# Token pairs for batch 0's V, heads paired two apart, and new orders of work in a fused attention and MLP kernel

## The chip, the cores and the metric

The kernel runs on one core of a Trainium2 chip. The metric is device time in microseconds. Before the change the median of three runs was 214.91 us (214.89 to 215.71). A core has a matrix engine (TensorE, PE in the profile; its weight loads are PEld), VectorE (DVE), ScalarE (ACT), GpSimd (POOL) and SyncE (SP). [...]

## The reference

Four batches, eight heads, 768 tokens, 64 elements a head. Tokens go in chunks of 32; a chunk's queries see 16 tokens to the left, the chunk, 8 to the right, and 8 memory tokens.

```python
for c in range(nc):
    q_c = q[:, :, c_start:c_end]
    k_full = concat([mem_k, k[:, :, l_start:r_end]]); v_full = ...
    a = softmax(scale * q_c @ k_full.T)
    out[:, :, c_start:c_end] = a @ v_full
x = out.transpose(0, 2, 1, 3).reshape(B * S, H * D)   # 3072 x 512
h = x @ w_in                                          # 512 x 2048
g = h + sin(alpha * h) ** 2 / (alpha + 1e-9)
return g @ w_out                                      # 2048 x 512
```

## The kernel before

**Stages.** A prologue (stage -1) does batch 0's attention; stages 0 to 3 then do the MLP of one batch each, and within stages 0 to 2 the next batch's attention. The order of all work is written by hand as strings of words (L813 for the prologue, L821 on for the stages); a word is a letter and its arguments, and `Stage.run` (L525) calls `do_<letter>`. The framework puts in the waits but moves nothing: every engine works its instructions in the order of the words. PSUM has 8 banks; `Banks` (L59) hands out pairs and single banks by the order in which they were given back.

**Blocks.** Three chunks make a block of 96 queries; a batch has 8 blocks. A block's keys are 128 rows: 64 tokens from 16 before the block, 8 memory tokens, 56 further tokens. For batches 1 to 3 the words are by block: `s` scores and exp (`scores`, L379), `v` values (`values`, L408) and normalizing (`normed`, L350), then the block's 96x512 result is turned for the MLP either by PE and a copy (`t` copy on DVE, `T` on ACT; `turned`, L362) or by a DMA transpose on SP's queue (`c`, L624).

**Batch 0** goes by head pair and half of the sequence instead (words `s01`, `v01`, `T01`: pair, half). k and q of two neighbouring heads at a time are loaded as f32 by eight DMAs on SP (L708), cast to bf16 by ACT or DVE (`a`, L653), transposed by PE (`k`, `l`; `turn`, L269) and copied into kT and qT (`K`, `L`; `put_k`, L282, with the sequence's two ends always by DVE, L291; `put_q`, L297). `u_scores` (L314) first puts the mask into PSUM with two 64x128x384 matmuls (L317) and then adds, per block, one matmul a head with 64 rows (the head's elements) and 128 columns (the keys) (L325); one 128x768 exp follows on ACT (L332). `u_values` (L339) multiplies the 128 keys by V with a column of ones (128x65, L344), the ones giving the softmax's sum. DVE takes the reciprocal (L353) and multiplies (L354); `u_turn` (L372) transposes four blocks of a pair by PE (L366) and copies them into xT (L369).

**V** lies in vw with a key on each partition: GpSimd loads it with 256 bytes a token and head, cast to bf16, as 64 token rows (L172) and 56 (L179), two to four heads at a time (`V`); the memory rows are loaded once for all batches (memv_st, L665, word `dm`) and copied into batch 0's V by DVE (`m0`, L188). GpSimd's DMAs use eight completion semaphores in turn, so its ninth waits until its first has landed.

**MLP.** `b` and `h` are the two halves of a tile of 128 of the 2048 hidden columns: four matmuls of 384 tokens each (`half_tile`, L422), over the four 128-row chunks of xT; then sine on ACT (L439), square on ACT, DVE or POOL (`q`, L441), gT on DVE (`g`, L451). The second product is fed in between, one 512-column matmul at a time (`f`, L462). `p` and `P` start a tile's first or second half early (`early`, L533). `I` and `U` load the weights, `R` and `X` a later batch's k and q by rows and their DMA transposes, `z` are fillers that keep PE busy, `W` loads ACT's table early, `C` sets up constants.

Of the kernel before, what the change touches and what calls it, by code (L numbers as in the profile page):

```python
# [17 lines left out]
ALU = mybir.AluOpType  # L18

# [66 lines left out]
def kernel(  # L86
# [42 lines left out]
    tiny = consts.tile([1, 1], F32, name="tiny")  # L129
    zeros = consts.tile([P, 512], BF, name="zeros")  # L130
# [3 lines left out]
    xslots = Slots([consts.tile([QW, HP, 2, D], BF, name=f"x_blk{i}") for i in range(6)])  # L134
    NPT = 8
    pts = [consts.tile([P, H * QW + 32], BF, name=f"pt{i}") for i in range(NPT)]
    memv_st = consts.tile([P, B, H, D], BF, name="memv_st")
    kst = consts.tile([P, NJ, H * D], BF, name="kst")
# [5 lines left out]
    memk_st = memv_st[96:104].rearrange("n b h d -> n b (h d)")  # L144
    memkT = consts.tile([P, HP, NK], BF, name="memkT")
# [13 lines left out]

    def load_v(b, h0, h1):  # L160
# [5 lines left out]
        lo = c0  # L166
        if c0 == 0 and b == 0:
            nc.gpsimd.dma_start(vw[16:64, 0:1, 0:D], vf[0:48, 0:1])
            lo = 1
        a = base + QW * lo - 16  # L170
        n = c1 - lo
        nc.gpsimd.dma_start(  # L172
            vw[0:64, lo:c1, 0:D], win(vflat, a, n, 64)
        )
# [94 lines left out]
    def turn(src, hp):  # L269
        bank, bs = banks.single()  # L270
        t = bank[:, 0:384].bitcast(BF).rearrange("p (r c) -> p r c", r=6)
        for r in range(6):
            for e in range(2):
                nc.tensor.transpose(
                    t[64 * e:64 * e + 64, r, :], src[:, 2 * hp + e, r, :], ident[:]
                )
        return t, bs

# [35 lines left out]
    def u_scores(b, hp, half):  # L314
# [7 lines left out]
        for i in range(4):  # L322
            j = 4 * half + i
            for e in range(2):
                nc.tensor.matmul(  # L325
                    t[:, e, QW * i:QW * i + QW],
                    kTs[b % 2][64 * e:64 * e + 64, hp, 104 * j:104 * j + P],
                    qTs[b % 2][64 * e:64 * e + 64, hp, QW * j:QW * j + QW],
                    start=False, stop=(i == 3),
                )  # L330
        pt = next_pt()
        nc.scalar.activation(  # L332
            pt[:, 0:H * QW].rearrange("p (e c) -> p e c", e=2), t[:, :, 0:HALF],
# [5 lines left out]
    def u_values(b, hp, half, pt):  # L339
        ot, bs = banks.pair()  # L340
        otv = ot[:, :, 0:4 * (D + 1)].rearrange("p e (g c) -> p e g c", c=D + 1)
        for e in range(2):
            for i in range(4):
                nc.tensor.matmul(  # L344
                    otv[:, e, i, :], pt[:, HALF * e + QW * i:HALF * e + QW * i + P],
                    vws[b % 2][:, 2 * hp + e, 4 * half + i, 0:D + 1],
                )
        return normed(otv, bs)

    def normed(otv, bs):  # L350
        rinv = blk.tile([QW, 2, HP], F32, name="rinv")
        x_blk = xslots.take()
        nc.vector.reciprocal(rinv[:], otv[0:QW, :, :, D])  # L353
        nc.vector.tensor_tensor(  # L354
            out=x_blk[:].rearrange("p g e d -> p e g d"), in0=otv[0:QW, :, :, 0:D],
# [4 lines left out]
        return x_blk  # L360
# [11 lines left out]
    def u_turn(xT, hp, half, x_blk, eng="V"):  # L372
        turned(
            x_blk,
            xT[:, hp, HALF * half:HALF * half + HALF].rearrange("p (g c) -> p g c", g=4), eng)
# [32 lines left out]
    def values(b, j, pt):  # L408
        ot, bs = banks.pair()
        otv = ot[:, :, 0:4 * (D + 1)].rearrange("p e (g c) -> p e g c", c=D + 1)  # L410
        for e in range(2):
            for hp in range(HP):
                i = 4 * e + hp
                nc.tensor.matmul(  # L414
                    otv[:, e, hp, :], pt[:, QW * i:QW * i + P],
                    vws[b % 2][:, 2 * hp + e, j, 0:D + 1],
                )
        return normed(otv, bs)
# [82 lines left out]
    todo = [(hp, half) for hp in range(HP) for half in range(2)]  # L501

    class Stage:
# [29 lines left out]
        def early(self, a, hf):  # L533
            if int(a) not in self.tile:
                self.tile[int(a)] = opened(int(a), self.next_x() if self.i < 0 else self.xT)
            t = self.tile[int(a)]
            half_tile(t, hf, 0, 3)
            t["from"][hf] = 3
# [46 lines left out]
        def do_k(self, a):  # L585
            self.piece["k" + a] = turn(k_bf, int(a))

        def do_l(self, a):
            self.piece["q" + a] = turn(q_bf, int(a))
# [13 lines left out]
        def do_v(self, a):  # L603
            if self.b == 0:
                self.xb[a] = u_values(0, int(a[0]), int(a[1]), self.pt.pop(a))
# [3 lines left out]
        def turn_x(self, a, eng):  # L609
            x = self.next_x()  # L610
            x_blk = self.xb.pop(a)
            if self.b == 0:
                u_turn(x, int(a[0]), int(a[1]), x_blk, eng)
            else:
                turned(x_blk, x[:, :, QW * int(a):QW * int(a) + QW], eng)
# [8 lines left out]
        def do_c(self, a):  # L624
            if self.b == 0:
                c0 = HALF * int(a[1])
                x = self.next_x()[:, int(a[0]), c0:c0 + HALF].rearrange("p (g c) -> p g c", g=4)
            else:
                c0 = QW * int(a)
                x = self.next_x()[:, :, c0:c0 + QW]  # L630
# [6 lines left out]
        def do_V(self, a):  # L637
            b, h0, h1 = (int(c) for c in a)
            load_v(b, h0, h1)

        def do_m(self, a):
            put_memv(int(a))

# [6 lines left out]
        def do_a(self, a):  # L650
            hp = int(a[0]) % HP
            dst = kq[int(a[0]) // HP]
            copier(a[1])(  # L653
                dst[:, 2 * hp:2 * hp + 2].rearrange("p h r d -> p h (r d)"), kq_f[int(a[0])][:]
# [8 lines left out]
        def do_d(self, a):  # L663
            if a == "m":
                nc.gpsimd.dma_start(memv_st[64:72].rearrange("n b h d -> n (b h) d"),  # L665
                                    mem_v.rearrange("b h n d -> n (b h) d"))
            elif a == "y":
# [5 lines left out]
            else:  # L673
                src, dst = (k, k_bf) if a[0] == "k" else (q, q_bf)
                load_one(src, dst, int(a[1]), int(a[2]), int(a[3]))
# [27 lines left out]
    kq_f = [mlp.tile([P, 2, 6 * D], F32, name="kq_f", tag=t) for t in ("u", "s2") * 4]  # L703
# [3 lines left out]
    def load_f(src, hp, t):  # L707
        nc.sync.dma_start(  # L708
            t[:], src[0, 2 * hp:2 * hp + 2].rearrange("h (p r) d -> p h (r d)", p=P)
        )  # L710

    load_f(k, 0, kq_f[0])
    load_f(q, 0, kq_f[4])
    for bb in range(B):
        if not CROSSED[bb][0]:
            nc.scalar.dma_start(memk_f[NM * bb:NM * bb + NM], mem_k[bb].rearrange("h n d -> n h d"))
    nc.scalar.dma_start(alpha_rows[:], moe_alpha.rearrange("(ft p) -> ft p", p=P))
    for hp in (1, 2, 3):
        load_f(k, hp, kq_f[hp])
        load_f(q, hp, kq_f[4 + hp])  # L720
    nc.vector.memset(zeros[:], 0.0)
    nc.vector.memset(tiny[:], 0.0)
    nc.vector.memset(mcol[:], 0.0)
    masks.make_identity(nc, ident[:])
    for vw in vws:
        nc.gpsimd.memset(vw[0:32, 0, 0, 0:D], 0.0)
        nc.gpsimd.memset(vw[96:128, H - 1, NJ - 1, 0:D], 0.0)
# [22 lines left out]
    def const_m():  # L750
# [3 lines left out]
        nc.vector.tensor_copy(mrow[:], mt)  # L754
# [11 lines left out]
    def const_k():  # L766
        nc.vector.tensor_copy(memk_bf, memk_f[0:NK])
# [30 lines left out]

    def const_v():
# [3 lines left out]
    def const_s():  # L803
# [4 lines left out]
                     s=const_s, z=const_z)  # L808
# [64 lines left out]
```

## Time and profile before

| | |
|---|---|
| median of three runs | 214.91 us |
| the profiled execution | 214.84 us, of which the span is 213.1 |
| TensorE clock granted | 1.0 |
| first MLP matmul (L424) of the unbroken stream | 24.81 us from the start |
| end of the last matmul group | 210.28 |
| DMA: software queue, hardware queue of SP | 13.25 MB in 68736 packets, 14.62 MB in 26976 |

A line of the page names an engine, an operation, the tiles it writes and reads, their shapes, and the number of instructions; behind the bar stand the time that the group was busy, the mean of one in ns, and the engine's idle time just before them with what ended it. A tile's name is that of the program. Slices are fortieths of the span, 5.3 us each, with the busy share in tenths. The chain of work is followed back from the end: each piece is what released the next one. In the DMA list the last number is the median from issue to landing.

### The profile page before, as it was taken

To read this page: it belongs to the slowest core of one execution; us is meant where nothing else is said; L and a number is where in the kernel's file an instruction comes from. 1 tells how busy PE (TensorE), PEld (TensorE's weight loads), DVE (VectorE), ACT (ScalarE), POOL (GpSimd) and SP (SyncE) were. 2 spreads that over 40 slices of the span, in tenths; PEclk is the share of its full clock that TensorE was granted. 3 is DMA by queue.
4 is the path that set the end of the run, shared out by engine and by line. 5 is a ranking of instruction groups with operands and counts; after the bars stand their busy time and mean duration, and the time that the engine had idled before them with its cause. 6 is when DMAs were issued, how large, how long until landed. Compare 5 with 4: busy or idle time off the path is not lost.

```text
span 213.1 us, 4479 instructions
## 1 busy us (share of the span) xinstructions
PE 201.7 (95%) x1721; PEld 113.5 (53%) x1721; DVE 140.5 (66%) x218; ACT 143.5 (67%) x230; POOL 99.8 (47%) x140
## 2 busy tenths in 40 slices
PE   0799899999999999999999999999999999999994
PEld 0456555565455556555455555554555555554443
DVE  7598678999542749975856649898157197865011
ACT  2597898976857469977846199887846289891110
POOL 8959515688598193009991039659400023200000
PEclk9999999999999999999999999999999999999999
DMA  6999999999999999969999229989945400000312
GB/s 195 337 163 141 193 209 205 204 163 182 131 177 141 137 148 144 180 88 110 126 217 171 72 63 131 156 126 129 175 115 123 124 15 0 2 3 0 148 49 98
DMA packets 95908, 28.19 MB, mean 132 GB/s; under 512 B 84864, under 2 KB 92432, under 8 KB 95888
## 3 DMA queue, kind: packets, MB, share of 16 engines
q0 software_dynamic: 68736, 13.25, 92.3%
q1 hardware_dynamic: 26976, 14.62, 28.2%
q8 instruction: 13, 0.21, 0.4%
q14 instruction: 7, 0.06, 0.1%
q10 hardware_dynamic: 176, 0.04, 0.1%
HBM read 29.66 MB, written 6.29 MB: 169 GB/s over the span
## 4 chain that ended last, share of the span: by engine, by line
PE 71%; DVE 9%; DMA 7%; ACT 4%; issue 4%; POOL 3%; DVEq 0%; POOLq 0%; ACTq 0%
PE ps L462 38%; PE ps L424 27%; DMA memv_st<-in_mem_v_dram 4%; DVE gT L451 4%; DVE s L447 3%; DMA vw<-in_v_dram 3%; PE ps L414 3%; PE ps L385 2%; ACT u L439 2%; PE ps L366 1%; ACT s L444 1%; POOL s L447 1%; POOL vw L172 1%; DVE kT L285 1%; ACT L699 1%
## 5 line engine op out<-in xcount | busy, mean ns | idle before, releaser
L462 PE MATMUL ps<-w_out_sb,gT 128*128 128x512 bf16 (+2 forms) x400 | 89.1, 371 | 0.0
L424 PE MATMUL ps<-xT,w_in_sb 128*128 128x384 bf16 x512 | 86.0, 326 | 0.7 <-DVE gT L451 0.4
L451 DVE SCALAR_TENSOR_TENSOR gT<-s,inv_alpha,ps 128x768 bf16<-128x768 f32 x64 | 63.0, 1011 | 12.5 <-ACT s L444 5.2
L424 PEld LDWEIGHTS <-w_in_sb 128*128 128x128 bf16 x512 | 49.8, 98 | 35.4 <-issue 2.1
L439 ACT ACTIVATE u<-ps,alpha_sb 128x768 f32<-128x768 f32 x64 | 56.6, 895 | 16.8 <-PE ps L424 14.3
L462 PEld LDWEIGHTS <-gT 128*128 128x128 bf16 x400 | 36.6, 98 | 37.9 <-DVE gT L451 0.2
L447 POOL TENSOR_TENSOR s<-u 128x768 f32<-128x768 f32 x11 | 17.4, 1582 | 69.7 <-ACT u L439 69.7
L399 ACT ACTIVATE pt<-ps,biasm 128x256 bf16<-128x256 f32 x72 | 27.2, 489 | 10.5 <-PE ps L385 10.5
L469 DVE COPY o_sb<-ps 128x512 f32<-128x512 f32 (+1 forms) x15 | 10.1, 678 | 28.3 <-PE ps L462 26.4
L447 DVE TENSOR_TENSOR s<-u 128x768 f32<-128x768 f32 x23 | 21.9, 953 | 7.8 <-ACT u L439 7.8
L444 ACT ACTIVATE s<-u 128x768 f32<-128x768 f32 x30 | 25.0, 841 | 0.5
L354 DVE TENSOR_TENSOR x_blk<-ps,rinv 96x512 bf16<-96x512 f32 x32 | 22.0, 687 | 1.1
L469 ACT COPY o_sb<-ps 128x512 f32<-128x512 f32 (+1 forms) x10 | 5.6, 562 | 21.6 <-PE ps L462 21.6
L172 POOL DMA_DIRECT2D vw<-in_v_dram x13 | 12.9, 994 | 7.9 <-PE ps L366 5.4
L353 DVE RECIPROCAL rinv<-ps 96x8 f32<-96x8 f32 x32 | 6.4, 200 | 13.5 <-PE ps L414 12.7
L179 POOL DMA_DIRECT2D vw<-in_v_dram x13 | 12.7, 976 | 0.0
L238 POOL DMA_DIRECT2D kst<-in_k_dram x16 | 12.2, 760 | 1.1 <-DMA vw<-in_v_dram 0.8
L232 POOL DMA_DIRECT2D kst<-in_k_dram x16 | 11.3, 708 | 2.3 <-DMA vw<-in_v_dram 1.6
L369 ACT COPY xT<-ps 128x384 bf16<-128x384 bf16 x12 | 5.6, 496 | 8.2 <-PE ps L366 8.2
L245 POOL DMA_DIRECT2D q_bf<-in_q_dram x12 | 10.7, 912 | 0.0
L414 PEld LDWEIGHTS <-pt 128*128 128x128 bf16 x192 | 8.2, 97 | 4.2 <-ACT pt L399 0.3
L414 PE MATMUL ps<-vw,pt 128*128 128x65 bf16 x192 | 8.9, 193 | 0.0
(81 smaller groups left out, 131.4 us busy)
## 6 DMA issues: line engine op xcount, KB each, us to landing
out_dram<-o_sb SPq DMA_DIRECT2D x23, 256.0 KB, 2.3
kq_f<-in_k_dram SPq DMA_DIRECT2D x4, 384.0 KB, 6.5
kq_f<-in_q_dram SPq DMA_DIRECT2D x4, 384.0 KB, 6.0
q_bf<-in_q_dram POOLq DMA_DIRECT2D x12, 128.0 KB, 6.7
w_in_sb<-in_moe_w_in_dram POOLq DMA_DIRECT2D x1, 1152.0 KB, 12.6
vw<-in_v_dram POOLq DMA_DIRECT2D x7, 128.0 KB, 6.7
vw<-in_v_dram POOLq DMA_DIRECT2D x8, 112.0 KB, 7.4
kst<-in_k_dram POOLq DMA_DIRECT2D x14, 64.0 KB, 5.1
```

What stands on the lines that cost most here:

```text
L172: nc.gpsimd.dma_start(vw[0:64, lo:c1, 0:D], win(vflat, a, n, 64))
L179: nc.gpsimd.dma_start(vw[72:128, c0:hi, 0:D], win(vflat, base + QW * c0 + 48, hi - c0, 56))
L354: nc.vector.tensor_tensor(out=x_blk[:].rearrange("p g e d -> p e g d"), in0=otv[0:QW, :, :, 0:D], in1=rinv[:].unsqueeze(3).to_broadcast([Q ...
L399: nc.scalar.activation(pt[:, 0:H * QW].rearrange("p (g e c) -> p g e c", g=2, e=4)[:, :, :, 32 * m:32 * m + 32], sc[:, :, 0:4 * QW].rearra ...
L414: nc.tensor.matmul(otv[:, e, hp, :], pt[:, QW * i:QW * i + P], vws[b % 2][:, 2 * hp + e, j, 0:D + 1],)
L424: nc.tensor.matmul(t["hT"][:, hf, 0:HALF], w_in_sb[:, kt, P * t["ft"]:P * t["ft"] + P], t["xT"][:, kt, HALF * hf:HALF * hf + HALF], start= ...
L439: nc.scalar.activation(t["u"][:], t["hT"][:, :, 0:HALF], ACTF.Sin, scale=alpha_sb[:, ft:ft + 1])
L444: nc.scalar.activation(s2[:], u[:], ACTF.Square)
L447: e.tensor_tensor(out=s2[:], in0=u[:], in1=u[:], op=ALU.mult)
L451: nc.vector.scalar_tensor_tensor(out=gT[:, ft, :].rearrange("p (e c) -> p e c", e=2), in0=t["s2"][:], scalar=inv_alpha[:, ft:ft + 1], in1= ...
L462: nc.tensor.matmul(o[:, c0:c1], gT[:, ft, P * s:P * s + P], w_out_sb[:, ft, c0:c1], start=(ft == 0), stop=(ft == FT - 1),)
L469: copier(state["engines"][state["o"] % len(state["engines"])])(o_sb[:, c0:c1], o[:, c0:c1])
```

## The change

- **First loads.** Only k and q of the first two pairs are still loaded as f32, k on SP's queue, q on ACT's; the memory keys and alpha move from ACT's queue to SP's. k and q of pairs 2 and 3 are loaded by GpSimd, cast on the way, into k_bf and q_bf (words `dq02 dk02 dk03 dq03`).
- **Pairs.** In batches 0 and 1 a pair is two heads two apart (`head`), so that two pairs make four neighbouring heads. The two cast pairs lie row by row, and `turn` needs six 128x128 transposes for them instead of twelve 128x64.
- **V of batch 0** has its own tile v0, in the memory of a gT buffer: on the partitions of one head's half (64) lie 64 pairs of keys; a row holds the even token, the odd token and 64 ones. GpSimd loads it with 512 bytes a descriptor, heads 0 to 3 first, the rest later. The memory rows come by a load of their own (`d0`) and are spread by eight small DMAs on SP (`N01`, `N23`), not by DVE. ACT writes the ones (`Co`).
- **Scores and values of batch 0.** For each block and head there are two score matmuls (even and odd keys, a stride of 2 in kT) with 64 rows and 64 columns, and two value matmuls with 64 rows, added in PSUM.
- **Turning batch 0.** Results of two pairs lie side by side; a `T` word does eight transposes and one 128x768 copy.
- **Orders.** All strings of words are new. The prologue ends with eight early MLP matmuls (`p12 p02 P12 P02`, the first two chunks of tiles 0 and 1). In stages 0 to 2 blocks turned by PE go from 5, 5, 0 to 2, 3, 1, those turned by DMA from 3, 3, 8 to 6, 5, 7.

The core of the diff:

```diff
+def head(b, u, e):
+    return 4 * (u // 2) + u % 2 + 2 * e if b < 2 else 2 * u + e
...
+    def load_v0(m, e, u0=0, u1=2):
...
+        nc.gpsimd.dma_start(
+            dst[64 * e:64 * e + 32, c0:n, 0:2 * D], rows(S * h0 + QW * c0 - 16, 32, n - c0)
+        )
+        nc.gpsimd.dma_start(dst[64 * e + 36:64 * e + 64, :, 0:2 * D], rows(S * h0 + 48, 28, n))
...
+    def put_memv0(u):
+        for e in range(2):
+            h = head(0, u, e)
+            nc.sync.dma_start(
+                v0[64 * e + 32:64 * e + 36, u, :, 0:2 * D],
+                memv0[:, h:h + 1, :].to_broadcast([4, NJ, 2 * D]),
+            )
...
         for i in range(4):
             j = 4 * half + i
-            for e in range(2):
-                nc.tensor.matmul(
-                    t[:, e, QW * i:QW * i + QW],
-                    kTs[b % 2][64 * e:64 * e + 64, hp, 104 * j:104 * j + P],
-                    qTs[b % 2][64 * e:64 * e + 64, hp, QW * j:QW * j + QW],
-                    start=False, stop=(i == 3),
-                )
+            for a in range(2):
+                for e in range(2):
+                    nc.tensor.matmul(
+                        t[64 * e:64 * e + 64, a, QW * i:QW * i + QW],
+                        kTs[b % 2][64 * e:64 * e + 64, hp, 104 * j + a:104 * j + P:2],
+                        qTs[b % 2][64 * e:64 * e + 64, hp, QW * j:QW * j + QW],
+                        start=False, stop=(i == 3),
+                    )
...
+        for i in range(4):
+            for a in range(2):
+                for e in range(2):
+                    rows = v0[64 * e:64 * e + 64, hp, 4 * half + i, :]
+                    both = rows.rearrange("p (x d) -> p x d", d=D)[:, 0:3:2, :]
+                    nc.tensor.matmul(
+                        otv[:, e, i, 0:D + 1] if a else otv[:, e, i, :],
+                        pt[64 * e:64 * e + 64, HALF * a + QW * i:HALF * a + QW * i + P],
+                        rows[:, D:2 * D + 1] if a else both,
+                        start=(a == 0), stop=(a == 1),
+                    )
...
+    for u in range(FP):
+        for c, src, eng in ((u, k, nc.sync), (HP + u, q, nc.scalar)):
+            kq_f[c] = mlp.tile([P, 2, 6 * D], F32, name="kq_f", tag=("u", "s2")[u % 2])
+            eng.dma_start(kq_f[c][:], of_pair(src, u))
...
+    def const_o():
+        nc.scalar.copy(
+            v0[:, :, :, 2 * D:3 * D].rearrange("p u j d -> p (u j) d"),
+            ones[:].unsqueeze(1).to_broadcast([P, HP * NJ, D]),
+        )
...
-        'a1A Cb Cp Cz Cv a5A eVA Cm Cl z4 a0V Ci k0 dm a4V l0 k1 K0V Ck l1 L0A V024 We L1V a2A K1A V002 '
-        'a6V k2 s00 K2V a3V s11 V068 m0 a7V s01 l2 s10 k3 K3A L2A V046 z4 v10 l3 Cs L3A I02 v11 s20 z1 '
-        'v01 s30 z1 v00 s31 z1 v30 s21 v31 T01 T10 v20 T30 T00 v21 T20 T31 I27 t11 t21 eVA Ws '
+        'Cb dq02 a0A z4 a4A Cm Cp k0 l0 Cz Ck K0A L0A Co a5V dk02 Ci s00 V00 d0 a1V l1 k1 Cl k2 K1A L1A eVA '
+        'l2 s01 dk03 N01 s11 s10 dq03 k3 l3 L2V K2V K3V L3A v00 s21 v10 s30 v01 I02 s20 N23 eVA v11 s31 dm '
+        'V01 Cs v30 T00 v20 T01 Cv v31 p12 v21 Ws p02 T10 T11 P12 I27 P02 '
...
-        'm1 s70 s3 f13 v0 f3 v6 c6 f6 v3 f5 s542 T3 f10 T0 v4 f6 v2 f2 v1 c4 c2 f7 v7 f1 T1 f3 v5 Ws T7 '
-        'f8 t5 '
...
+        'f6 c6 v3 f4 s542 t3 f10 v4 f2 c0 v2 v1 f5 c4 v7 c2 v5 f8 T1 c7 Ws c5 f11 '
```

The last two groups are the end of stage 0's words, before and after.

More of the change, by code (lines that the diff above doesn't have):

```diff
@@ L370, in turned, with u_turn @@
         banks.give(bs)
[L372 to L375, printed above, removed]
+    def u_turn(xT, m, half, xq, eng="V"):
+        bank, bs = banks.single()
+        xtp = bank[:, 0:4 * QW].bitcast(BF).rearrange("p (e g c) -> p e g c", e=2, g=4)
+        for e in range(2):
+            for g in range(4):
+                nc.tensor.transpose(
+                    xtp[:, e, g, :], xq[:, e, g].rearrange("p a d -> p (a d)"), ident[0:QW, 0:QW]
+                )
+        copier(eng)(
+            xT[:, 2 * m:2 * m + 2, HALF * half:HALF * half + HALF]
+            .rearrange("p e (g c) -> p e g c", g=4), xtp)
+        banks.give(bs)
     def scores(b, js):
```

187 lines of the change are left out of this document (113 added, 74 removed), and 34 rows, old and new, of the table stage.

## The prediction

> **What bounds the kernel now.** I read the page's busy shares and slices first. All times are us from the start of the span.
>
> ```profile
> PE 201.7 (95%) x1721; PEld 113.5 (53%) x1721; DVE 140.5 (66%) x218; ACT 143.5 (67%) x230; POOL 99.8 (47%) x140
> ...
> PE   0799899999999999999999999999999999999994
> ```
>
> PE is full in every slice but the first few and the last. So only three things can move the end: when the unbroken PE stream starts, how much PE work is in it, and holes torn into it. Next I read the chain of work that ended last, for the start of the stream:
>
> ```profile
> 4.86 9.20 DMA memv_st<-in_mem_v_dram
> 14.06 0.28 issue
> 14.34 1.75 POOL vw L172
> 16.09 6.06 DMA vw<-in_v_dram
> 22.29 0.43 PE ps L344 x8
> 23.05 0.70 DVE x_blk L354
> 23.79 0.70 PE ps L366 x12
> 24.55 0.48 ACT xT L369
> ```
>
> The prologue (batch 0's attention) ends with V: GpSimd's ninth load waits until memv_st, its first, has landed at 14.06, and the last values wait for that V. Then the timeline, where the stream begins:
>
> ```profile
> 23.89 0.69 DVE L354 TENSOR_TENSOR x_blk<-ps,rinv 96x512 bf16<-96x512 f32 x1
> ...
> 24.81 17.62 PE L424 MATMUL ps<-xT,w_in_sb 128*128 128x384 bf16 x104
> ```
>
> From 24.81 on PE's starts show eight holes of 0.2 to 0.4, 2.2 in all. From here each microsecond earlier is one off the end. Last, the groups kept apart by shape, for prices:
>
> ```profile
> L332 ACT ACTIVATE pt<-ps 128x768 bf16<-128x768 f32 x8 | 6.3, 811 | 1.3 <-PE ps L325 1.3
> L369 ACT COPY xT<-ps 128x384 bf16<-128x384 bf16 x12 | 5.6, 496 | 8.2 <-PE ps L366 8.2
> L366 PE MATMUL ps<-ident,x_blk 96*128 96x96 bf16 x72 | 5.4, 206 | 0.7 <-DVE x_blk L354 0.6
> L344 PE MATMUL ps<-vw,pt 128*128 128x65 bf16 x64 | 3.4, 193 | 0.4 <-DMA vw<-in_v_dram 0.2
> L325 PE MATMUL ps<-qT,kT 64*128 64x96 bf16 x64 | 2.8, 203 | 0.0
> ```
>
> A matmul's mean holds its pipeline; spacing of starts is what costs. In the timeline, L325's two heads start 3 ns apart and pairs 40 ns apart; L344 follows every 32; L424 every 163 (56 in 9.11); four L366 take 0.28.
>
> **The change, part by part.**
>
> *First loads.* Eight f32 tiles on SP land at 4.61, 5.76, 7.28, 8.34 and so on to 14.41 (landing events). Now k0 and q0 start together on SP and ACT: I take the second landing, 5.7, for both, the fourth, 8.4, for k1 and q1. Pairs 2 and 3 come by GpSimd, cast on the way: four casts (L653, 0.5 to 0.83) vanish from DVE and ACT.
>
> *ACT's chain.* Two casts at 0.83 from 5.7: 7.4. K0, L0 (0.72, 0.80): 8.9. New is the copy of ones into V's third block, 128x2048, which no row shows: from 384 columns (0.50) to 768 (0.82) is 0.85 ns a column, so 1.9; bounds 0.8 (the 768-wide row) and 2.7 (2048/384 times 0.50). I take 1.9, the slope: 10.8. First exp 0.8, K1, L1 1.5: 13.1. By then DVE has cast q1 and k1 (0.75, 0.55 after 8.4).
>
> *DVE's chain.* Its copy of K1's ends (L291, 0.26) stands in its queue behind ACT's K1 at 12.3, and L2, K2, K3 behind it: 12.4 + 0.95 + 0.85 + 0.26 + 0.85 + 0.26 = 15.5. Here normalizing can begin: eight times reciprocal and multiply, 0.20 + 0.69, spaced 0.87, so 22.5 at the earliest. Before, the first stood at 16.56 and the last ended at 24.58. The 8-partition V-memory copy (L188, 1.22) leaves DVE; SP's eight small DMAs take its place.
>
> *GpSimd's queue.* Before the first V load (5.75) it gains two k/q issues, about 0.65 each (between L168's 0.56 and L155's 0.91), and loses memv_st (0.90), the ones of V (0.65) and two fills (0.28): V's first half, five issues, goes out from 5.2 to 9.0, its memory rows to 9.5, k3 and q3 to 10.85. Landing of an unqueued load takes 2.7 (49 KB row of V), of a queued one 6.7 (128 KB row). I take 2.7 to 3.3, because V of batch 0 has half the packets (512 B read where it was 256 B) and SP's f32 loads, which held memv_st back for 9.20, are half: q3 at 13.5, memory rows at 12.0, and their SP copies, 0.45 to issue and 2.0 to land (1.6 to 2.4 by SP's other rows), at 14.3. V's second half, behind w_in's first columns and memv_st, is issued 12.5 to 15.9 and lands at 18.6, needed at 18.5. Behind the memory rows' wait SP has nothing but their own eight copies until the first output.
>
> *PE.* k3 and l3 end at 14.0, first values at 14.3. A unit of values is now 16 matmuls in 8 pairs of heads, 128 and 65 columns: 8 x 0.043 + 0.13 between groups = 0.47 (was 0.38); scores are 0.17 for the masks + 8 x 0.040 + 0.13 = 0.62 (was 0.46). Behind 14.3 stand 8 values, 4 scores, two groups of eight transposes (0.45) and two early matmuls: 3.8 + 2.5 + 0.9 + 0.3 = 7.5, interleaved with waits for DVE, so the last values end at 22.0, normalized 22.9, transposed 23.4. ACT, after the other exps, the T00 and T01 copies (0.82 each, ending 21.5) and the table load (1.28 + 0.20), copies T10 and T11 by 24.6. Then h0 runs, with ten of the stream's L424 already done (eight early ones, two of b0): 24.6 - 10 x 0.163 = 22.97 against 24.81: **-1.84**.
>
> *The stream.* Transposes by PE fall from ten to six (stages 0 to 2: five, five, none to two, three, one): 16 x 0.07 = **-1.12**. The same blocks go by DMA, 14 to 18, on SP. Their landing depends on the stage:
>
> ```profile
> xT<-x_blk SPq DMA_TRANSPOSE x3, 4.2
> ...
> xT<-x_blk SPq DMA_TRANSPOSE x8, 2.4
> ```
>
> These are the DMA issues of 105 to 123 (stage 1's end; stage 0's answer has the same row) and of 150 to 170. In stage 0 block 5's matmuls are now followed by f8, T1, f11, b0, then h0, which needs it: 0.25 + 1.73 + 0.28 + 2.38 + 0.65 = 5.3. Block 7's transpose holds SP (1.2), so block 5's is issued at 1.9 and lands at 1.9 + 4.2 = 6.1: **+0.8**. In stage 1 the last is issued 1.0 after its values and has 5.5: free. Batch 1's k and q ride behind w_in: its second part is issued at 17.6 (before 18.81), lands at 23.9 (4.06 of flow, as from 22.66 to 26.72 before, from 19.8 on), and the queue needs 15.8 more to the last of k and q (26.72 to 42.46): 39.7. PE asks for it at 42.35 - 1.84 = 40.5: free, with 0.8 to spare.
>
> Holes from the other new orders: bounds -1.0 (most of today's holes) and +1.5; I take 0.
>
> Sum: 214.84 (the profiled execution: span 213.1 and 1.74 around it) - 1.84 - 1.12 + 0.8 = **212.7**. The median of the runs shown is 214.91, 0.07 from it.
>
> [...] In L325 the two heads write different banks; now they sit in opposite quarters of the array and write the same bank's two halves. L274's column halves also write one bank and start 1 to 3 ns apart, 52 ns a pair. [...]
>
> **The rivals.**
>
> A, the sum: 212.7, from 211.5 to 213.7. Chance 0.50.
>
> B, score pairs do not overlap: 80 ns a pair for 40, 0.32 a unit, four units behind 14.3: +1.3, 214.0. [...] Against: L274, L325. Chance 0.08.
>
> C, the prologue stays bound by landings, and the change does not do what it says: GpSimd's loads still crawl beside SP's and ACT's f32 loads. With q3 landing 4.7 to 6.7 after issue, first values come at 15.7 to 17.4, the stream 1.2 to 2.7 later: 213.9 to 215.4, say 214.7. For: memv_st's 9.20. Against: half the f32 loads. Chance 0.18.
>
> D, slower: DMA transposes come late at both stage ends. L633's longest landing is 6.1. Then stage 0 waits 1.9 + 6.1 - 5.3 = 2.7, stage 1 1.0 + 6.1 - 5.5 = 1.6: 214.84 - 2.96 + 4.3 = 216.2. It decides once both waits exceed 2.96 together. For: GpSimd's loads of batch 2 run in those very windows. Against: the median. Chance 0.12.
>
> E, better: block 5 lands in 2.4 and some holes close: 211.5. Chance 0.12.
>
> **How the numbers follow.** Likeliest A: 212.7. For 8 in 10 the range reaches over C, E and half the way to D: 211.2 to 215.6. About 0.5% (1.07) is what a measurement can tell here. Faster by more: A, E, and a little of B and C: 0.64. Within: B and C's rest: 0.23. Slower: D and C's end: 0.13.
>
> **What would show it.** The first L424 after all four 128x768 xT copies at about 24.6, with eight L424 before; first reciprocal near 15.5; ones copy near 1.9; score pairs at 40 ns (B: 80); q3 landing near 13.5 (C: 15 or more); a hole of 0.8 ahead of h0 in stage 1 (D: over 2). I am wrong if first values wait for a DMA beyond 15.5, or if the later stages hold new holes of more than 1.5 in all.

## The result and the profile after

The changed kernel took 237.32 us (median of four runs, 235.68 to 238.28) where the kernel before took 215.31 (214.89 to 216.75): a ratio of 1.100, with an interval of 1.092 to 1.108. The prediction, 212.7 and a range up to 215.6, was wrong by sign and by far: 22 us slower. Ratios and their intervals are of fast runs alone, medians of all runs. The profiled execution took 237.11, with a span of 235.1.

First the page's busy shares, the slices (5.9 us each) and the granted clock of TensorE:

```profile
PE 211.3 (90%) x1802; PEld 118.1 (50%) x1802; DVE 137.8 (59%) x215; ACT 142.4 (61%) x221; POOL 101.2 (43%) x144
...
PE   3875999999899689999269999999999999999995
...
PEclk9998899999999979999959999999999999999999
```

PE is no longer full. Three places give way: slices 2 and 3 (about 12 to 24 us, the prologue), slice 13 (76 to 82, the end of stage 0) and slices 19 and 20 (112 to 123, stage 1). The row of the clock dips behind each of them. PE's busy sum rose by 9.6: it has 81 more matmuls (the scores and values of batch 0 are now two for one), and at half clock the same work takes longer: L493 starts every 320 ns from 83.6 to 86.1, at 0.5, and every 163 from 86.3 on, at 1.0.

Next, the four greatest of PE's waits between 14 and 125 us (engine and line, what it waited for, us in total, times, longest):

```profile
PE ps L451 <- DMA qT<-q_bf: 6.3, 2, 5.7
PE ps L402 <- DMA gT<-kst: 4.6, 3, 3.4
PE ps L493 <- DMA xT<-x_blks: 2.6, 1, 2.6
PE ps L451 <- ACT pt L465: 1.0, 1, 1.0
```

The first three are the three places (a tile is named by the memory that it lies in: the memory rows in a kst buffer, v0 in a gT buffer): batch 2's q transposes in stage 1, the small copies of memory rows in the prologue, and the DMA transposes of the last blocks at the end of stage 0. The timeline has them in place:

```profile
15.91 0.50 PE L326 MATMUL ps<-ident,q_bf 128*64 128x128 bf16 x12
19.82 0.21 PE L402 MATMUL ps<-gT,pt 64*128 64x128 bf16 x1 [3.41 <-DMA gT<-kst]
20.68 0.47 PE L402 MATMUL ps<-gT,pt 64*128 64x128 bf16 x14 [0.64 <-DMA gT<-kst]
...
27.18 0.50 PE L402 MATMUL ps<-gT,pt 64*128 64x128 bf16 x15 [0.54 <-DMA gT<-kst]
...
31.39 0.52 PE L435 MATMUL ps<-ident,x_blks 96*128 96x96 bf16 x8 [0.25 <-DVE x_blks L413]
31.74 1.54 PE L493 MATMUL ps<-xT,w_in_sb 128*128 128x384 bf16 x8
...
83.05 7.20 PE L493 MATMUL ps<-xT,w_in_sb 128*128 128x384 bf16 x34 [2.61 <-DMA xT<-x_blks]
...
118.98 0.50 PE L451 MATMUL ps<-qT,kT 64*128 64x96 bf16 x8 [5.69 <-DMA qT<-q_bf]
```

The last transposes of the prologue (L435) begin at 31.39; before, the last (L366) began at 24.63:

```profile
24.63 0.34 PE L366 MATMUL ps<-ident,x_blk 96*128 96x96 bf16 x4 [0.15 <-DVE x_blk L354]
```

For the prologue's delay the chain of work says what made it (start, us, what):

```profile
8.99 5.29 DMA kst<-in_mem_v_dram
14.29 0.02 issue
14.30 0.82 SPq L207
...
18.60 0.64 SPq L207
19.24 0.04 issue
19.29 7.76 DMA gT<-kst
27.05 0.14 issue
27.18 0.52 PE ps L402 x8
```

The load of the memory rows lands at 14.29. Behind it SP issues the eight copies one after another. Landing events: the first is there at 19.69, 5.4 after its issue, then 20.55, 20.73, 20.90, 21.88, 23.79, 25.24, 27.05. So a copy takes from 4.3 us (the fourth, issued at 16.56) to 7.8 (the eighth). The first two make the values start at 19.82 and 20.68; the eighth, which the values of the second two pairs wait for, sets the end of the prologue.

To see how much each place costs I compared, for every kernel, the times at which PE had done the same amount of MLP matmuls (L493 and L531; L424 and L462 before). The difference from the profiled execution before I call the **lag**. In us, at 10, 35, 40, 65, 70 us of such work and at the end (a few records are missing from traces, so late values hold to some 0.3):

| kernel | 10 | 35 | 40 | 65 | 70 | end | time |
|---|---|---|---|---|---|---|---|
| after | 6.9 | 9.3 | 11.8 | 11.8 | 21.0 | 22.0 | 237.11 |
| e1_x6_up | 6.0 | 8.4 | 10.8 | 10.9 | 11.6 | 12.6 | 227.69 |
| e2_pe_end | 7.2 | 9.7 | 9.6 | 9.4 | 18.9 | 19.1 | 234.34 |
| e3_memv_first | 3.2 | 5.6 | 7.8 | 8.3 | 17.7 | 18.4 | 233.49 |
| e4_old_orders | 5.5 | 5.5 | 5.5 | 5.5 | 9.2 | 9.2 | 224.54 |
| e5_fill | 5.4 | 7.9 | 10.0 | 10.1 | 19.2 | 19.3 | 234.39 |
| e6_memv_dve | 4.3 | 6.8 | 7.8 | 7.6 | 16.8 | 17.0 | 231.87 |
| e7_all | 3.8 | 6.3 | 6.2 | 6.0 | 6.7 | 8.3 | 223.52 |
| e9_first_old | 1.8 | 1.8 | 1.8 | 1.8 | 1.8 | 1.8 | 216.88 |
| e12_first_old_timed | 4.3 | 4.3 | 4.3 | 4.3 | 4.3 | 4.3 | 219.48 |

So of 22.0 us the prologue makes 6.9, stage 0 up to its end 2.4, the passage to stage 1 2.5, the hole in stage 1 9.2, and the rest 1.0. The 2.4 and the 2.5 belong together: at 35 the new orders have done all 64 value matmuls of batch 1 and the old ones 24 of them, 40 at some 32 ns, so about 1.3 of the 2.4 is work done earlier and comes back at 40. What is lost by 40 is a wait of 1.0 for ACT's exp, the hole of 2.6 and half clock behind it. Each experiment takes one of these away or all of the new orders.

### The profile page after: what moved, and what is told of

It reads as the page before. It is cut to its first block, busy times and chain, and to the rows that moved or that the text cites. A ratio compares the mean times of both kernels' runs of the same rounds, so it can differ in the third digit from the quotient of the medians.

```text
span 235.1 us, 4653 instructions
## 1 busy us (share of the span) xinstructions
PE 211.3 (90%) x1802; PEld 118.1 (50%) x1802; DVE 137.8 (59%) x215; ACT 142.4 (61%) x221; POOL 101.2 (43%) x144
## 4 chain that ended last, share of the span: by engine, by line
PE 54%; DMA 14%; POOL 10%; DVE 6%; ACT 5%; issue 5%; SPq 4%; POOLq 0%; DVEq 0%; ACTq 0%
PE ps L531 26%; PE ps L493 23%; DMA qT<-q_bf 5%; DMA gT<-kst 3%; ACT u L508 3%; POOL s L516 2%; DVE x_blks L413 2%; DMA kst<-in_mem_v_dram 2%; POOL vw L241 2%; SPq L207 2%; DMA xT<-x_blks 2%; SPq L309 2%; DVE gT L520 2%; DMA q_bf<-in_q_dram 2%; PE ps L451 2%
## 5 line engine op out<-in xcount | busy, mean ns | idle before, releaser
L493 PE MATMUL ps<-xT,w_in_sb 128*128 128x384 bf16 x512 | 88.5, 330 | 4.1 <-DMA xT<-x_blks 2.6
L531 PE MATMUL ps<-w_out_sb,gT 128*128 128x512 bf16 (+2 forms) x400 | 90.2, 376 | 0.0
L493 PEld LDWEIGHTS <-w_in_sb 128*128 128x128 bf16 x512 | 50.0, 98 | 40.8 <-issue 7.8
L531 PEld LDWEIGHTS <-gT 128*128 128x128 bf16 x400 | 37.2, 99 | 39.8 <-issue 2.3
L516 POOL TENSOR_TENSOR s<-u 128x768 f32<-128x768 f32 x12 | 19.4, 1625 | 76.9 <-ACT u L508 76.9
L516 DVE TENSOR_TENSOR s<-u 128x768 f32<-128x768 f32 x25 | 23.8, 958 | 18.4 <-ACT u L508 18.4
L538 DVE COPY o_sb<-ps 128x512 f32<-128x512 f32 (+1 forms) x15 | 10.1, 682 | 36.2 <-PE ps L531 36.2
L513 ACT ACTIVATE s<-u 128x768 f32<-128x768 f32 x27 | 22.8, 843 | 0.6
L413 DVE TENSOR_TENSOR x_blks<-ps,rinv 96x512 bf16<-96x512 f32 x32 | 22.0, 686 | 1.1
L412 DVE RECIPROCAL rinv<-ps 96x8 f32<-96x8 f32 x32 | 6.4, 199 | 18.9 <-PE ps L481 11.7
L218 POOL DMA_DIRECT2D vw<-in_v_dram x9 | 8.4, 935 | 15.3 <-PE ps L481 15.3
L451 PE MATMUL ps<-qT,kT 64*128 64x96 bf16 x192 | 6.7, 209 | 7.5 <-DMA qT<-q_bf 6.3
L387 ACT ACTIVATE pt<-ps 128x768 bf16<-128x768 f32 x8 | 6.4, 810 | 8.4 <-PE ps L380 8.3
L451 PEld LDWEIGHTS <-kT 64*128 64x128 bf16 x192 | 4.8, 96 | 11.9 <-issue 10.4
## 6 DMA issues: line engine op xcount, KB each, us to landing
w_out_sb<-in_moe_w_out_dram POOLq DMA_DIRECT2D x6, 128.0 KB, 15.4
```

Source lines behind the costliest of these rows:

```text
L413: nc.vector.tensor_tensor(out=out, in0=otv[0:QW, :, :, 0:D], in1=rinv[:].unsqueeze(3).to_broadcast([QW, 2, HP, D]), op=ALU.mult,)
L451: nc.tensor.matmul(sc[:, e, QW * hp:QW * hp + QW], kTs[b % 2][64 * e:64 * e + 64, hp, pitch * j:pitch * j + P], qTs[b % 2][64 * e:64 * e + ...
L493: nc.tensor.matmul(t["hT"][:, hf, 0:HALF], w_in_sb[:, kt, P * t["ft"]:P * t["ft"] + P], t["xT"][:, kt, HALF * hf:HALF * hf + HALF], start= ...
L513: nc.scalar.activation(s2[:], u[:], ACTF.Square)
L516: e.tensor_tensor(out=s2[:], in0=u[:], in1=u[:], op=ALU.mult)
L531: nc.tensor.matmul(o[:, c0:c1], gT[:, ft, P * s:P * s + P], w_out_sb[:, ft, c0:c1], start=(ft == 0), stop=(ft == FT - 1),)
```

## The experiments

Lines are those of the changed kernel. "Old orders" are the strings of words of stages 0 to 3 of the kernel before, which the changed kernel can run as they are; its prologue's words stay new. Single times are of one run; where a ratio stands, it is from rounds beside the kernel before on the same chip. The kernel before, run once beside e1 to e4, took 220.96, and once beside e5, e6, e7 and e9, 219.26, where its median is 215.31: a difference of a few us between two single times shows little by itself. The argument rests on the waits, landings and lags in the traces.

### e1_x6_up: the q transposes ahead of the store

Why did q's transposes come late? This is SP's queue in stage 1, before and after (each line is a group; the us include waits within it):

```profile
91.58 8.49 SPq L263 DMA_TRANSPOSE qT<-q_bf  x6
104.71 0.93 SPq L472 DMA_DIRECT2D out_dram<-o_sb  x2
```

```profile
88.44 12.70 SPq L306 DMA_TRANSPOSE kT<-kst  x8
106.59 0.34 SPq L541 DMA_DIRECT2D out_dram<-o_sb  x1
107.03 10.07 SPq L309 DMA_TRANSPOSE qT<-q_bf  x6
```

Before, q's six followed k's eight at once. In both orders the word for q, `X6`, stands some twenty words behind `X8`; but the old one feeds 15 second products in between (`f8 f7`), the new one 27 (`f11 f10 f6`), and every 16 end in a store of the output. So a store came between: it waited until 106.59 for its tile, 5.4 us of idle queue, and q's transposes waited behind it.

```diff
- 'g4 R1 q6A ... q10A X8 V226 '
- '... f6 b15 V202 X6 q13V f2 ... '
+ 'g4 R1 q6A ... q10A X8 X6 V226 '
+ '... f6 b15 V202 q13V f2 ... '
```

> Only one word moves: in stage 1 the six DMA transposes of batch 2's q (X6) follow directly on the eight of k (X8), ahead of an output store. Theory 'orders' (the largest hole, PE idle from 113 to 119 and at half clock until 123.7, comes because SP's queue holds those six behind a store that waits for PE and ACT until 106.6): the hole goes, about 9 us with its half clock, 228 (226.5 to 229.5). Rival 'late flow' (q's transposes are late because the loads and k's transposes before them are late, after the prologue's 6 us): k's transposes end at 101 anyway, q's last lands hardly sooner, 4 us of hole at least stay: 232 or more.

Measured 227.69, 9.4 less. SP's queue now:

```profile
87.07 13.09 SPq L306 DMA_TRANSPOSE kT<-kst  x8
100.25 7.87 SPq L309 DMA_TRANSPOSE qT<-q_bf  x6
108.20 8.31 SPq L541 DMA_DIRECT2D out_dram<-o_sb  x3
```

q's transposes end at 108.1 instead of 117.1, PE has no wait for them, and the lag grows by 0.7 from 65 to 70 where it grew by 9.2. One word in another place was worth 8.5 us (9.2 less 0.7; the other 0.9 of the 9.4 lies in the prologue, where the eighth copy landed at 25.04 in this run): one store at the head of the queue, 6.3 us of PE's waits, and the half clock behind them.

### e2_pe_end: stage 0's end turned by PE

```diff
- '... v5 f8 T1 c7 Ws c5 f11 '
+ '... v5 f8 T1 Ws T7 f11 t5 '
```

> Stage 0's last two blocks, 7 and 5, are turned by PE and a copy instead of DMA transposes. Theory 'orders': the wait of 2.8 ahead of stage 1's first h0 and the half clock behind it (1.6) go, eight transposes (0.6) come: 3.8 faster at stage 1's start; if the later hole (113 to 124) keeps its size, 233.3 at the end. Rival 'late flow': q's transposes of stage 1 come when they come, so what is gained here is waited for there, and the end stays at 236 to 237.

Measured 234.34, 2.8 less. At the end of stage 0 the changed kernel's queue of SP had a store ahead of the transposes of blocks 7 and 5:

```profile
76.80 0.34 SPq L541 DMA_DIRECT2D out_dram<-o_sb  x1
77.23 2.50 SPq L704 DMA_TRANSPOSE xT<-x_blks  x2
```

Here both blocks are turned by PE. The wait for the DMA transposes is gone, with two small ones for copies in its place:

```profile
78.31 0.33 PE L424 MATMUL ps<-ident,x_blks 96*128 96x96 bf16 x4 [0.56 <-ACT xT L427]
78.48 2.54 PE L531 MATMUL ps<-w_out_sb,gT 128*128 128x512 bf16 x11
80.86 0.34 PE L424 MATMUL ps<-ident,x_blks 96*128 96x96 bf16 x4
81.03 0.82 PE L493 MATMUL ps<-xT,w_in_sb 128*128 128x384 bf16 x4
82.07 8.14 PE L493 MATMUL ps<-xT,w_in_sb 128*128 128x384 bf16 x49 [0.23 <-DVE xT L427]
```

What was won here was not lost at the later hole: the lag falls by 2.2 at 40 and by 2.9 at the end.

### e3_memv_first: the memory rows loaded first

```diff
- 'Cb dq02 a0A ... s00 V00 d0 a1V ... '
+ 'Cb d0 dq02 a0A ... s00 V00 a1V ... '
```

> The load of batch 0's memory rows is GpSimd's first load instead of its eighth; nothing else moves. If the first values waited for the late landing of those rows (14.3), SP's eight copies start at about 6 and the first values come at 16.5, bound by the last k and q: PE does not idle 3.6 us, its clock is not halved at 21, the stream starts 4 to 5 earlier, and the end is near 232.5 if that gain is kept. [...] Rival 'late flow': all later holes shrink with the prologue, the end falls by more than 6.

Measured 233.49. The first values start at 16.87 instead of 19.82, no half clock follows in the prologue, and the lag at 10 is 3.2 instead of 6.9. With the rows in early the copies are no longer waited for, slow as they still are (3.1 to 5.7 us in e9, which has the same prologue). What waits next in the prologue is V's second half:

```profile
16.87 0.52 PE L402 MATMUL ps<-gT,pt 64*128 64x128 bf16 x16
...
22.50 0.52 PE L402 MATMUL ps<-gT,pt 64*128 64x128 bf16 x15 [0.90 <-DMA gT<-in_v_dram]
```

### e6_memv_dve: the copies by VectorE

```diff
-            nc.sync.dma_start(
+            nc.vector.tensor_copy(
                 v0[64 * e + 32:64 * e + 36, u, :, 0:2 * D], ...
- '... dk03 N01 s11 ... L3A v00 ... s20 N23 eVA v11 s31 dm '
+ '... dk03 s11 ... L3A N01 v00 ... s20 eVA v11 N23 s31 dm '
```

> The changed kernel, but VectorE copies the memory rows to their four-partition places in the value tile, two copies ahead of the first values and two ahead of the values of the other u, instead of SyncE's eight transfers. Theory 'copies' (the transfers' 5.5 to 7.8 us to land are the wait of the prologue, the load of the rows only its smaller part): the rows are there at 14.3 us, the first values start at 16.5 to 17.5 instead of 19.8, no half clock near 21 us, the stream's offset against the kernel before falls from 6.4 to 2.5 to 3.5 us, time 233 to 234. Rival 'the rest of the prologue is late anyway' (value rows landing, VectorE's casts behind the copies, GpSimd's flow): first values earlier but the stream starts less than 1.5 us earlier, time 236 or more.

Measured 231.87. The values start at 17.8, and there is no half clock in the prologue. The wait has moved to the copies on DVE (the first four, of 4x1024 elements, take 2.08 us from 17.34 on), and I had put the second four too late:

```profile
PE ps L402 <- DVE gT L207: 3.9, 4, 1.7
```

Even so the lag at 10 is 2.6 less than after's. Both e3 and e6 say the same from two sides: rows at 14.3 and copies of 4.3 to 7.8 us behind them (the recorded 5.5 to 7.8 leaves out the faster ones) are together the prologue's late start; taking away either one removes most of it.

### e5_fill: zeros while PE waits

```diff
- '... K3V L3A v00 ... '
+ '... K3V L3A z14 v00 ... '
```

> The changed kernel with one word more in the prologue: 14 matmuls of zeros stand on TensorE ahead of the first values, where it stood idle from 16.2 to 19.8 us, so that it is busy while it waits for the copied memory rows; nothing is waited for earlier. Theory 'two costs' (the wait itself, and the half clock that follows an idle TensorE by a period of 3.41 us): the first values still start at 19.8 us, no granted clock of 0.5 stands near 21 to 25 us, and the stream of the MLP starts about 1.7 us less late, since half a period's work is not lost: offset of the stream 4.7 us where it was 6.4, time 235.4. Rival 'the clock there costs nothing' (the values and scores of the prologue wait for VectorE, ScalarE and landings in any case): the half clock is gone or not, and the offset stays within 0.5 us of 6.4, time 237.

Measured 234.39, 2.7 less. The windows show the same 3.4 us of the changed kernel and of this one (columns: the window, its length, busy us and instructions of PE, PEld, DVE, ACT and POOL, then TensorE's granted clock, DMA share and GB/s):

```profile
21.30:24.70 3.40, 3.40 (x70) 2.74 (x68) 1.77 (x4) 1.49 (x2) 1.88 (x4) 0.50 1.16 209
```

```profile
21.30:24.70 3.40, 3.40 (x109) 2.60 (x103) 2.85 (x7) 2.43 (x3) 1.71 (x3) 1.00 1.18 212
```

With PE kept busy on zeros the clock stays at 1.0 and 109 instead of 70 matmuls pass. The lag at 10 falls by 1.5, as theory 'two costs' has it, but the clock isn't shown to be the reason. In this run the memory rows landed at 13.11 instead of 14.29, and the eighth copy at 25.00 instead of 27.05. From the chain of work:

```profile
9.02 4.09 DMA kst<-in_mem_v_dram
...
18.14 6.85 DMA gT<-kst
```

The changed kernel's chain waits for that copy until 27.05 whatever the clock did before, so an earlier landing alone can give the 1.5. e4, whose prologue has the same words as the changed kernel's, has no half clock there, and no fillers: its eighth copy lands at 25.66, 1.39 earlier than the changed kernel's, and its lag at 10 is 1.4 less. So no price of the half clock in the prologue is shown, and these two runs leave nothing for it. (e1, with half clock there and its eighth copy at 25.04, has 0.6 more lag at 10 than e5.)

### e7_all: three repairs, new orders kept

The diffs of e1, e2 and e3 together.

> The changed kernel with three repairs at once, its new orders otherwise kept: memory rows loaded first on GpSimd's queue, the last blocks of stage 0 turned by TensorE as in the kernel before, and the transposes of q for batch 2 issued in stage 1 ahead of the store. By themselves they gave 3.6, 2.8 and 9.4 us of the 237.1. Theory 'three separate holes': the gains add up, 220.5 to 222, that is 5.5 to 7 above the kernel before, which stand in the prologue (2.7) and in small holes of the new orders. Rival 'what is won is waited for elsewhere' (an earlier stream meets transposes, casts and stores that are not earlier): the sum falls short by over 2 us, 223.5 or more, with a new hole in stage 0 or 1.

Measured 223.52: the rival's bound. The gains of the three add up to 15.8 and 13.6 arrived. No new hole as large as the three appears, so the rival's condition did not come. What is missing has two parts. The prologue is 0.6 later than e3's (3.8 for 3.2): PE waited 1.4 for V's second half, and half clock followed from 24.20 to 27.61. Behind the prologue stand many small waits between 30 and 200 us that the old orders don't have, the greatest

```profile
PE ps L451 <- ACT pt L465: 1.0, 1, 1.0
...
PE ps L424 <- ACT xT L427: 0.6, 1, 0.6
PE ps L493 <- DVE o_sb L538: 0.5, 1, 0.5
```

and its lag grows by 4.5 behind the prologue, where e9's doesn't grow at all. PE's idle time in the stream is 2.8 more than before; the rest of the 4.5 is not accounted for.

### e4_old_orders, e9_first_old, e8_dve_old: the new parts with the old orders

```diff
- for i, words in enumerate((( 'I7g b0 h0 b1 q0V ...   # the new strings of stages 0 to 3
+ for i, words in enumerate((( 'o8 b0 h0 I7g q0V ...   # those of the kernel before
```

e9 adds e3's diff, e8 adds e6's.

> The changed kernel with the words of stages 0 to 3 from before; prologue as changed. Theory 'orders': only the prologue's loss (6.4 to 6.9 later at the same MLP work) is left: 221.7 (220.5 to 223). Rival 'late flow': a late prologue shifts loads and transposes against PE in these orders too, holes of several us at stage ends: 226 or more.

> The changed kernel's parts with the kernel before's orders of stages 0 to 3, and the load of the memory rows issued first on GpSimd's queue: the new layout alone, with the prologue's worst wait shortened. Theory 'orders and one wait' (what the layout itself costs is the late start of the stream, +2.7 us as in the run with the load first; the hole of 2.0 us with its half clock at 107.5 in the run with the old orders comes from something else of the orders and stays): offset 2.7 minus the transposes that the layout saves, then about 3.7 at that hole: 220 to 221. Rival 'the hole at 107.5 was made by the late start' (the transposes of q wait for a queue that is late against TensorE's clock after the stall): it goes with the late start, and the time is 216.5 to 218.

> The changed kernel with the kernel before's orders of stages 0 to 3, and with VectorE copying the memory rows into the value tile in place of SyncE's eight transfers; their load stays where the change put it. It stands between two runs: with the late prologue (stream 5.5 us late) the old orders had a hole of 2.0 us and a period of half clock at 107.5; with the load first (1.8 us late) they had none. Theory 'lateness feeds the hole' (SyncE's fourteen transposes for batch 2, 1.3 us each, keep a slack of a few us that a late prologue eats): offset 3 to 3.5 us at the start, no hole over 1 us at 107, no half clock, 217.5 to 218.5. Rival 'GpSimd's order of loads makes the hole' (the load of the memory rows between the value loads, as in the run with the hole): a hole of 1.5 to 2 us again, 220.5 to 222.

e4 took 224.54: between the two theories. Its lag is 5.5 from the prologue on and stays so to the decimal through stage 0, and one hole of 1.9 with a period of half clock is left:

```profile
107.33 0.34 PE L451 MATMUL ps<-qT,kT 64*128 64x96 bf16 x8
109.52 0.35 PE L451 MATMUL ps<-qT,kT 64*128 64x96 bf16 x8 [1.85 <-DMA qT<-q_bf]
```

By the times the new orders cost 12.6 of the 22; by the growth of the lag behind the prologue (15.1 in the changed kernel, 3.7 in e4) 11.4, since e4's prologue, with the same words, came out 1.4 shorter. e9 took 216.88, as the rival had it: no such hole, lag 1.8 throughout. e8 took 220.37, by its time nearer to the rival; but it has no hole there and no half clock, and what it lost it lost in the prologue: its last L435 begin at 29.52, e4's at 30.01, e9's at 26.28. So the place of the load doesn't make the hole: e8 has it where e4 has, and a prologue only 0.5 less late. In e4's queue of SP the first transpose of k waited longer for SP's copy of memory rows into kst (4.7 us; 3.1 before, 3.5 in e8, 3.7 in e9, 4.0 in e12):

```profile
SPq L306 <- DMA kst<-memv_st: 4.7, 1, 4.7
```

Fourteen transposes follow it, 19.4 us in a row, and the last is needed as it lands. From the issue of that copy to the first transpose 6.3 us passed in e4 and 4.6 in e8, 1.7 more, the order of the hole (1.85); that it was this landing is argued from the traces, not shown by a run.

### e10_v_up, e11_early and e12_first_old_timed: can the new parts win?

e10 issues V's second half earlier (`v01 I02 s20 ... dm V01 Cs` becomes `v01 V01 I02 s20 ... dm Cs`), on top of e9. e11 has besides: k of the second pair loaded ahead of the small loads, the ones copied by DVE, and a prologue in another order (`a5V`, `l1` and `L1A` ahead of `s00`; `v00` ahead of `k3 l3`). e12 is e9 again, timed. The end of e11's prologue against that of the changed kernel:

```diff
- 'dq03 k3 l3 L2V K2V K3V L3A v00 s21 v10 s30 v01 I02 ... '
- 'V01 Cs v30 ... '
+ 'dq03 L2V K2V v00 k3 l3 K3V L3A s21 v10 s30 v01 V01 I02 ... '
+ 'Cs v30 ... '
```

> As the run with the load first and the old orders (216.88), and on GpSimd's queue batch 0's second half of V is issued ahead of the first columns of w_in and of the memory rows of the other batches. Theory 'one wait left' (the values of the second half waited 1.1 us for their landing at 21.75, and the four normalizings at 0.93 us each, the last transposes and the stream follow them one to one): the landing comes at about 20.3, no wait on PE at 20.7, the stream 1.1 us earlier, 215.5 to 216.0, ratio to the kernel before 1.00 to 1.01. Rival 'w_in is late instead' (the stream's first matmuls wait for columns issued 2.8 us later): a new hole near 24 us and 216.9 or more.

> As the run with V up, and the whole prologue tightened: k of the second head pair is loaded before the small loads on SyncE's queue, the copy of ones is made by VectorE while it stands idle near 4 to 6 us instead of by ScalarE ahead of its first exponential, q of the second pair is cast, turned and copied before the first scores, and the first values stand ahead of the last k and q transposes. Theory 'TensorE's own work bounds the middle of the prologue' (it was nearly unbroken from 8.8 to 20.7 us): it reaches the second half of the values 0.7 to 1.2 us earlier, V by then lands at about 20, so 0.3 to 0.8 us more are won, 214.8 to 215.5, within 0.3% of the kernel before. Rival 'landings bound it': no gain over the run with V up, since the second half of V lands at the same time: 215.5 to 216.

> The kernel with the load of the memory rows first and the old orders once more, timed in five rounds, since its one time (216.88) stood beside a single run of the kernel before that was 4 us above its median. Theory 'the layout itself costs a little' (without the new orders' holes and the memory rows' wait the stream still starts 1.8 us late, by the landing of V's second half): 216.5 to 217.5 where the kernel before has its 215 to 216, ratio 1.005 to 1.012. Rival 'the layout gains once the holes are gone' (as its terms in the prediction would have it, -1.84 in the prologue): ratio below 1.00.

| kernel | median | before, same chip | ratio | interval |
|---|---|---|---|---|
| e10_v_up | 219.47 | 216.34 | 1.018 | 1.009 to 1.026 |
| e11_early | 219.08 | 216.34 | 1.012 | 1.007 to 1.018 |
| e12_first_old_timed | 219.20 | 216.20 | 1.013 | 1.008 to 1.017 |

None beats the kernel before, and the three can't be told apart. The times are above what e10's theory and both readings of e11 gave; e10's rival has the time (216.9 or more) but not the mechanism: its trace shows no wait for w_in. What they all left out is that e9's landings were good ones. e12 is the same program on another chip, and its last L435 begin at 28.83 instead of 26.28, with no other difference up to the end. q of the last pair landed at 17.04 there and at 15.86 in e9 (issued at the same 10.4), the last of V's second half at 23.37 and 21.75. PE's waits in e12's prologue:

```profile
PE ps L326 <- DMA k_bf<-in_k_dram: 1.0, 1, 1.0
PE ps L402 <- issue: 1.0, 1, 1.0
PE ps L402 <- DVE x_blks L413: 0.8, 1, 0.8
PE ps L326 <- DMA q_bf<-in_q_dram: 0.7, 1, 0.7
PE ps L402 <- DMA gT<-in_v_dram: 0.4, 1, 0.4
```

So the new prologue lives on landings that differ by 1 to 2 us between executions, and the lags at 10 of e3, e5 and e6 hold no better than that. Whether it is the chip is open: e12's six runs on one chip reach from 217.47 to 220.03. In e10 the second half of V landed at 21.86 and the last L435 began at 27.38, 1.45 ahead of e12's; the medians don't show it. In e11 they began at 28.01: no gain over e10, as its rival had it; the last of V's second half landed at 21.45. The wait put down to "issue" (a group of values broken off after 11 of 16 matmuls for 1 us, also in e3, e10 and e11) has no releaser in the trace; its cause is open.

## Why the prediction was wrong

Step by step, as the prediction put them.

- **First loads, ACT's chain.** Right where they could be seen: the first two tiles land at 5.3 and 5.7 (5.7 said); the copy of ones took 1.90 (1.9, by the slope of the shorter copies). k1 came at 9.4 and q1 at 6.8 for 8.4.
- **GpSimd's queue: the step that failed first.** "Memory rows at 12.0, and their SP copies, 0.45 to issue and 2.0 to land, at 14.3." The rows landed at 14.29; one issue took 0.64; a landing took 4.3 to 7.8. The first values started at 19.82 for 14.3, and the eighth copy landed at 27.05, so that the stream, forecast 1.84 earlier, came 6.9 later. Two prices were wrong. GpSimd's landings were taken at 2.7 to 3.3, from a load at 60 to 76 us, while V's loads in the trace before took 6.1 to 9.4 in the prologue; 4.3 to 6.8 were measured for batch 0's V, the rows, k3 and q3. And the 1.6 to 2.4 by which I priced the copies are of SP's output stores and of transposes late in the kernel; a nearer row, SP's own copy within SBUF (kst from memv_st), made the next transpose wait 3.1 in the trace before. At its landing the semaphore of the second copy, to four partitions, rises in four steps (20.12, 20.36, 20.48, 20.55), that of the memory rows' load in 16 (12.90 to 14.29). Whether this goes with the slow landings no run shows; their shape alone doesn't set them: in e9 the same copies, issued from 7.29 on, took 3.1 to 5.7. The prediction gave this step no bounds, and its rows were from another neighbourhood.
- **k3, q3 and V's second half.** 13.5 and 18.6 said; 15.4 and 21.0 measured. This is rival C, held at 0.18 and priced at 2.0. With the rows first and the old orders its landings are the larger part of PE's waits that remain (2.1 of 3.9 us in e12's list), and 2.7 to 3.1 us against the kernel before remain in rounds.
- **PE in the prologue.** Score pairs do start 40 ns apart at full clock (from 15.09; 80 at half clock, from 21.29), the two heads 3 ns apart, on one bank: rival B is out. From the first values to the end of the last transposes the prediction had 9.1 (14.3 to 23.4); e9 took 10.3 (16.36 to 26.63), 1.1 of it waiting. So this part was sized rightly; it started late.
- **Transposes, -1.12.** Their number fell as said (24 L424 in six groups). At the price of 0.07 each the gain is there, under the rest; no run measures it apart.
- **Block 5 at stage 0's end: +0.8.** The mechanism was right, the size not. I had block 5's transpose issued 1.9 after its values; it was issued 3.2 after (78.52), since an output store held SP until 76.80 and block 7's transpose went only at 77.23. The landing took 4.4 (4.2 said). The hole was 2.6, near the price rival D had put on it (2.7), but by luck: D had it from a landing of 6.1, and it was the issue that came late. D's second hole, at stage 1's end, did not come.
- **"Holes from the other new orders: bounds -1.0 and +1.5; I take 0."** The step that made the result wrong. e4 puts the new orders at 11.4 to 12.6 us. The bounds were taken from the holes the kernel before has, as if new orders could only shift those; what I did not do is follow SP's queue through stage 1 word by word, where a store stands between `X8` and `X6` and 14 transposes of some 1.3 us follow one another.
- **A cost not in the sum at all: the clock.** The trace before shows 1.0 throughout, so I priced no hole above its own length. After has half clock at 21.29 to 24.71, 82.73 to 86.15 and 116.87 to 123.69, in periods of 3.41 us; PE was busy for 10.6 of these 13.7 us, so at most 5.3 are lost. In e4 the price can be read: a hole of 1.85 and one period of half clock made the lag grow by 3.7. The periods in after all start on one grid of 3.413 us. In the windows of that grid just ahead of 21.29, 82.73 and 116.87 PE was busy for 0.82, 1.11 and 0.00 us. It need not be so little: here are the windows just ahead of a half clock in e4 and in e7 (columns as in e5), with 1.57 and 1.99 us of busy PE.

```profile
106.85:110.27 3.42, 1.57 (x22) 0.72 (x21) 1.98 (x3) 2.91 (x6) 3.42 (x6) 1.00 2.16 132
```

```profile
20.79:24.20 3.41, 1.99 (x59) 1.53 (x56) 1.54 (x3) 1.40 (x3) 2.83 (x4) 1.00 1.21 206
```

  Busy time alone doesn't decide either: e6's window from 21.01 to 24.42 has 1.91 and full clock behind it. And e6 has a hole of 2.4 at the end of stage 0 (77.89 to 80.28) and no half clock behind it, where after has one behind its 2.6. Counted on by 3.413 from 21.01, a border of e6's grid at 79.04 cuts its hole in two, and PE is busy for 2.2 of either window; in after's, ahead of 82.73, for 1.11. That it matters where a hole falls on the grid is my reading of these two; no run shows it apart.

## What to carry to other kernels

When a hand-made order changes, follow each in-order queue through the new order, DMA issues included: one output store that waited for its tile held six transposes for 5 us and cost 8.5. A hole of PE is to be priced at its length and, for each period of half clock that follows, up to half of 3.41 us, 1.7 (L493 started every 320 ns for 163); in these runs a period followed holes of 1.4 (e7) and 1.9 (e4) and did not follow one of 2.4 (e6), so bound it both ways. A landing time is to be taken from rows with the same neighbours and the same number of partitions (the copies' 2.0 came from others; they took 4.3 to 7.8), and a repair that changes landings too (e5) shows nothing until the landings are set side by side.

## What was not expected of the hardware

- Copies of 8 KB within SBUF to four partitions took 4.3 to 7.8 us to land beside GpSimd's loads (3.1 to 5.7 when issued 7 us earlier, in e9), and 0.64 each to issue. The same rows copied by VectorE took 0.5 each.
- Half clock followed windows of 3.41 us in which TensorE was busy for 1.57 (e4) and 1.99 us (e7).
- Two executions of one program (e9 and e12) differ by 2.5 us at the end of the prologue: landings of loads, and a break of 1 us without a releaser.
